# A fused attention, mixture-of-experts and GLU kernel: where the row list of the first expert is made

## The chip, the cores and the metric

The kernel runs on one core of one Trainium2 chip. The metric is the device time of one execution in microseconds (us). A core has a matrix engine (PE in the profile, with its weight loads as PEld), a vector engine (DVE), a scalar engine (ACT), GpSimd (POOL) and SyncE (SP), each with an instruction stream of its own. DMAs can be issued from the queues of SP, ACT and POOL.

## The reference

Inputs are q, k, v of 4 x 8 heads x 576 x 64, so 2304 tokens with 512 features. Everything is float32.

```python
kv  = einsum('bhsd,bhse->bhde', k, v)
x   = rmsnorm(einsum('bhsd,bhde->bhse', q, kv)) * g_norm   # 2304 x 512
noisy = x @ w_gate + log1p(exp(x @ w_noise)) * noise       # 8 experts
top2, weights = the two largest, softmax over these two
out[token] += weight * (relu(x @ w1[e]) @ w2[e])           # w1 512x1024, w2 1024x512
y = (sigmoid(out @ m2_gate) * (out @ m2_val)) @ m2_out     # width 1536
```

## The kernel before

The 2304 tokens are 18 tiles of 128. The attention stage makes one tile after the other; its raw rows go to a DRAM buffer `xbuf`. Routing is done for groups of tiles, `GROUPS = [(0, 5), (5, 8), (8, 13), (13, 18)]`: group 0 and 1 are "first", group 2 is `third` in the code, group 3 is `last`.

**The list.** Each token goes to two experts and has in each a slot number: a block `sb` (a column of 40, 5 blocks x 8 experts) and a place `rm` of 128 in the block. To gather the rows of a block, the kernel needs the list "which token stands at which place". It makes it by matmuls: for each tile i and choice j a one-hot `ohs[:, i, j]` (128 tokens x 128 places, by `rm`; this is the wide one) is multiplied with a one-hot `ovs[:, i, j]` (128 tokens x 40 columns, by `sb`) that has been multiplied with the token's number. The sum over all tiles in PSUM (`plist`) is the list; with a constant added it becomes `lsb`, whose columns are the row numbers of the indirect DMAs (`gather`). Both one-hots lie in one float16 tile, called `ohv` in the trace. A first, small list (`pfirst`, `lsa`) of groups 0 and 1 alone serves the first two blocks (`AB = 2`) of expert 0, so that expert 0 can begin while groups 2 and 3 are still routed. A third form, `lsq`, has four row numbers for each place (rows as quarters); it is made from the whole list by a copy (`lsf`), four small matmuls (`psq`) and one addition, and is what the gathers for expert 1 from its third block on and for all later experts read.

**Routing as a generator.** `route(g)` is cut by `yield` into 19 steps, for group 3: 1 is `rms_a`; 2 is ACT's Ln and Exp; 3 to 5 finish the norm `rms_y`, copy it beside the rows (POOL for group 3) and store rows; 6 and 7 are the logits (`Lr`, `lg`); 8 is ACT's Exp and Ln (`sp`); 9 to 11 find the two largest (`mk`); 12 and 13 rank them (`prk` on PE); 14 gives `sb` and `rm`; 15 to 17 make the one-hots; 18 and 19 the token's weights. `step(g, n)` runs n steps of group g at that place of the program, `advance(n)` n steps of all groups in work.

**Weight splits.** Weights are split in a high part (ACT) and a low part (DVE, which subtracts ACT's result). `work()` does the next split and loads the next raw weights: for expert 0, four pieces of w1 (`w_0h`, `w_0l` to `w_3h`, `w_3l`), then four of w2 of the same names. Each w1 piece is used by one call `h_first(p, 0)`, which multiplies the first two blocks (256 rows) with 256 columns of w1 in 24 matmuls (`ph`) and leaves the relu in high and low parts (`ha`; ACT, then DVE). Then two calls of `y_step` (24 matmuls each, `py`) multiply with w2, then the three blocks 2 to 4 come in: gather, scaling (`xs`, DVE), four transposes each (`pxT`), high part `xh` (ACT) and low part `xl` (DVE), and the second half of the first layer (`ph` with 368 columns).

**Order.** SP and POOL keep program order everywhere, ACT does up to the end of this part; PE and DVE are ordered by a scheduler from the program's priorities, except inside the `with in_order("PE DVE")` block, whose PE and DVE instructions keep their order among themselves. Steps of groups 1 and 3 have a higher priority (`URGENT`).

Before the block, PE does four idle products (`warm`, eight instructions) while the first gathers land. `free` holds tiles for split weights.

## Time and profile before

| | before |
|---|---|
| median of 3 runs | 944.24 us (944.13 to 947.38) |
| the profiled execution | 937.66 us |
| span of its instructions | 935.9 us |
| mean granted clock of PE | 0.996 |
| PE busy | 909.1 us (97%) |
| DVE busy | 682.3 us (73%) |
| ACT busy | 439.6 us (47%) |
| POOL busy | 383.6 us (41%) |

A row of the timeline gives start, duration, engine, line of the kernel, operation, what it writes and reads, and in brackets how long the engine had been idle before it and what ended that. Durations of neighbours on one engine overlap a little, so the cost of one among many is the distance of starts.

### The profile page before, as it was taken

The numbers are of one execution on the slowest core, as the hardware profiler recorded it, in microseconds if no ns is written. First come the engines' busy times: TensorE is split into PE (matmuls) and PEld (weight loads), VectorE is DVE, ScalarE is ACT, GpSimd is POOL, SyncE is SP. The second block draws the span as 40 slices with busy tenths as digits, with TensorE's granted clock in tenths as the row PEclk, the third lists the DMA queues.
The fourth block names the chain that finished last, engine by engine and source line by source line (L and its number), as shares of the span: only waits on it lengthen the run. The fifth ranks groups of instructions, "written<-read, shape, count | busy, mean of one in ns | idle before, by whom it ended". The sixth has DMA issues, their size and how long they took to land.

```text
span 935.9 us, 14318 instructions
## 1 busy us (share of the span) xinstructions
PE 909.1 (97%) x5157; PEld 788.7 (84%) x5157; DVE 682.3 (73%) x1025; ACT 439.6 (47%) x659; POOL 383.6 (41%) x378
## 2 busy tenths in 40 slices
PE   7888889999999999999999999999999999999998
PEld 4877779989798998989899898888888888888886
DVE  2489597877788687787967468987977767866463
ACT  1675254353434343424333687554654555544441
POOL 2142664737366383844600383333453636300000
PEclk9999999999999999999999999999999999999999
DMA  9986678777857566666744476696477777986784
GB/s 263 290 257 216 188 216 279 259 257 274 262 188 234 185 221 194 207 206 216 225 155 141 140 251 215 217 333 222 171 266 263 244 253 252 350 269 201 217 249 98
DMA packets 134379, 213.92 MB, mean 229 GB/s; under 512 B 20384, under 2 KB 65952, under 8 KB 134304
## 3 DMA queue, kind: packets, MB, share of 16 engines
q1 hardware_dynamic: 116496, 179.82, 59.7%
q0 software_dynamic: 7664, 20.26, 7.4%
q10 hardware_dynamic: 10144, 12.88, 4.1%
q8 instruction: 41, 0.67, 0.3%
q14 instruction: 34, 0.28, 0.1%
HBM read 140.94 MB, written 71.97 MB: 228 GB/s over the span
## 4 chain that ended last, share of the span: by engine, by line
PE 58%; DVE 5%; DMA 4%; ACT 2%; issue 2%; SPq 1%; POOL 0%; DVEq 0%; ACTq 0%
PE py L817 15%; PE ph L774 14%; PE pga L1174 8%; PE poa L1353 7%; PE pgc L1174 4%; PE poc L1353 3%; PE pgb L1174 2%; PE pout L1323 2%; PE pob L1353 2%; DMA xturn<-yg 1%; DMA yg<-ybuf,slot 1%; DVE wt L994 1%; DMA lw<-wbuf 1%; DMA yg<-xturn 1%; DVE xf L1072 1%
## 5 line engine op out<-in xcount | busy, mean ns | idle before, releaser
L714 POOL DMA_INDIRECT xg<-xbuf,lsq x132 | 152.8, 1158 | 51.2 <-issue 30.9
L994 DVE TENSOR_TENSOR wt<-lw,wt 128x512 fp32r<-128x512 f32 x84 | 69.9, 837 | 35.7 <-ACT wt L993 33.6
L778 ACT ACTIVATE hh<-ph 128x624 fp32r<-128x624 f32 (+1 forms) x60 | 41.4, 694 | 95.7 <-PE ph L774 93.9
L779 DVE SCALAR_TENSOR_TENSOR hl<-ph,hh 128x624 fp32r<-128x624 f32 (+1 forms) x60 | 48.7, 811 | 48.2 <-ACT hh L778 47.0
L714 POOL DMA_INDIRECT yg<-ybuf,slot x36 | 39.0, 1084 | 77.6 <-issue 57.7
L733 POOL TENSOR_TENSOR xg<-xg 128x512 f32<-128x512 f32 x33 | 36.5, 1107 | 40.3 <-DMA xg<-xbuf,lsq 35.2
L763 ACT ACTIVATE xh<-xT 128x512 fp32r<-128x512 f32 (+3 forms) x40 | 21.1, 543 | 66.6 <-DVE xT L760 65.4
L993 ACT ACTIVATE wt<-lw 128x512 fp32r<-128x512 f32 x84 | 49.9, 621 | 0.0
L1211 POOL TENSOR_TENSOR qt<-qv 128x512 f32<-128x512 f32 x12 | 19.7, 1642 | 68.9 <-DVE qv L1198 37.2
L1188 ACT ACTIVATE q<-pga 128x1024 f32<-128x1024 f32 x24 | 24.6, 1027 | 44.8 <-PE pga L1174 43.5
L764 DVE TENSOR_TENSOR xl<-xT,xh 128x512 fp32r<-128x512 f32 (+3 forms) x40 | 24.9, 634 | 27.0 <-ACT xh L763 27.0
L695 POOL COPY seen<-hh 128x1 f32<-128x1 f32 x42 | 16.8, 401 | 65.7 <-ACT hh L778 65.5
L774 PE MATMUL ph<-xh,w_3h 128*128 128x312 f32 (+2 forms) x128 | 39.3, 307 | 1.6 <-DVE hl L779 0.9
L774 PE MATMUL ph<-xh,w_3l 128*128 128x312 f32 (+2 forms) x128 | 39.3, 307 | 1.5 <-DVE w_3l L645 1.5
L774 PE MATMUL ph<-xl,w_0h 128*128 128x312 f32 (+2 forms) x128 | 39.1, 313 | 1.3 <-DVE xl L764 1.3
L822 ACT ACTIVATE yo<-py 128x512 f32<-128x512 f32 (+1 forms) x40 | 23.5, 588 | 35.6 <-PE py L817 32.7
L774 PE MATMUL ph<-xh,w_1l 128*128 128x312 f32 (+2 forms) x128 | 39.2, 307 | 0.7 <-DVE w_1l L645 0.7
L774 PE MATMUL ph<-xh,w_0l 128*128 128x312 f32 (+2 forms) x128 | 39.6, 312 | 0.3 <-PEq L852 0.3
L774 PE MATMUL ph<-xh,w_0h 128*128 128x312 f32 (+2 forms) x128 | 39.6, 312 | 0.0
L774 PE MATMUL ph<-xh,w_1h 128*128 128x312 f32 (+2 forms) x128 | 39.2, 306 | 0.0
L774 PE MATMUL ph<-xl,w_2h 128*128 128x312 f32 (+2 forms) x128 | 39.1, 306 | 0.0
L774 PE MATMUL ph<-xh,w_2h 128*128 128x312 f32 (+2 forms) x128 | 39.1, 306 | 0.0
(562 smaller groups left out, 3118.5 us busy)
## 6 DMA issues: line engine op xcount, KB each, us to landing
raw<-in_moe_w_dram SPq DMA_DIRECT2D x60, 512.0 KB, 4.8
lw<-wbuf SPq DMA_DIRECT2D x84, 256.0 KB, 4.1
gr<-qbuf SPq DMA_DIRECT2D x42, 512.0 KB, 4.7
ybuf<-yo ACTq DMA_DIRECT2D x32, 256.0 KB, 3.2
ybuf<-zero SPq DMA_DIRECT2D x29, 256.0 KB, 6.3
raw<-in_moe_w_out_dram SPq DMA_DIRECT2D x12, 512.0 KB, 5.5
raw<-in_moe_w_gate_dram SPq DMA_DIRECT2D x12, 512.0 KB, 4.8
raw<-in_moe_w_val_dram SPq DMA_DIRECT2D x12, 512.0 KB, 4.4
```

Of the source, the lines that this page charges most:

```text
L714: nc.gpsimd.indirect_dma_start(out=x, out_offset=None, in_=src, in_offset=bass.IndirectOffsetOnAxis(ap=ix, axis=0))
L733: eng.tensor_mul(xv, xv, x[:, :, 128:, None].to_broadcast([128, 4, KD, 32]))
L764: nc.vector.tensor_sub(XL[e, s][:, :, a:z], pt[:, :, o:o + z - a], XA[e, s][:, :, a:z].bitcast(FT))
L774: nc.tensor.matmul(ph, w[:, c, j], x[e, s][:, c, :], start=(n == 0), stop=(n == 3 * KD - 1))
L778: nc.scalar.activation(hh, ph, AF.Relu)
L779: nc.vector.scalar_tensor_tensor(hl, ph, 0.0, hh.bitcast(FT), op0=OP.max, op1=OP.subtract)
L817: nc.tensor.matmul(py[0:m], x[:, f % 2, t], w[:, f % 2, :], start=(n == 0), stop=(n == 3 * FC - 1))
L993: nc.scalar.activation(hi, src, AF.Copy)
L994: nc.vector.tensor_sub(lo, src, hi.bitcast(FT))
L1174: nc.tensor.matmul(ps[:, j, 0:HT[c]], w[:, a, k, s], x[:, k, :], start=(first and i == 0), stop=(i == 5), skip_group_check=not first)
L1188: nc.scalar.activation(q[name], src, AF.Copy)
L1353: nc.tensor.matmul(ps[:, j, 0:HT[c]], w, g[x][1][:, f, :], start=(first and u + f + i == 0), stop=(u == FP3 - 1 and f + i == 3), skip_grou ...
```

## The change

Four edits. (1) The token's number is multiplied into the wide one-hot `ohs` as the second operation of the instruction that makes it; the multiplication of `ovs`, an instruction of its own, goes. (2) The last group's wide one-hots are all made on DVE; before, three of the ten were POOL's. (3) In the program's order, the split of w1's second piece moves ahead of `step(third)` and the first steps of the last group inside the block, and the split of its fourth piece moves from behind `h_first(1, 0)` and steps 8 to 11 of the last group to ahead of them. In the same place step 8 of the last group moves behind `h_first(1, 0)`. (4) `lsf`, `psq` and `lsq` are made together with `lsb`, at its priority, before the rows of blocks 2 to 4 are scaled and brought in; before, they stood behind that.

```diff
@@ route
-                eng = nc.gpsimd if j and (g != len(groups) - 1 or i < 3) or not g else nc.vector
-                eng.tensor_scalar(ohs[:, i, j], i128[:, 0:128], rm[:, i, j:j + 1], None, op0=OP.is_equal)
+                eng = nc.gpsimd if j and g != len(groups) - 1 or not g else nc.vector
+                eng.tensor_scalar(ohs[:, i, j], i128[:, 0:128], rm[:, i, j:j + 1], tokid[:, t0 + i:t0 + i + 1],
+                                  op0=OP.is_equal, op1=OP.mult)
             if i == 1:
                 nc.vector.tensor_tensor(ovs[:, :n], i128[:, None, None, 0:NB * E].to_broadcast(shp),
                                         sb[:, :, :, None].to_broadcast(shp), op=OP.is_equal)
-                nc.vector.tensor_mul(ovs[:, :n], ovs[:, :n], tokid[:, t0:t1, None, None].to_broadcast(shp))
@@ main program
         nc.tensor.matmul(pw, qT[NT - 1][:, 0], qT[NT - 1].rearrange("p h d -> p (h d)"), start=True, stop=True)
+        work()
         step(third)
-        step(last, 2)
-        work()
-        step(last)
+        step(last, 3)
         h_first(0, 0)
     work()
     step(third)
     step(last, 4)
     step(third, 2)
-    step(last)
+    work()
     h_first(1, 0)
-    step(last, 3)
+    step(last, 4)
     step(third)
-    work()
     h_first(2, 0)
@@
         for blk in range(AB, NB):
             gather(0, blk)
+        lsf = sml.tile([128, NB * E], HF, name="lsf")
+        nc.vector.tensor_copy(lsf, pl)
+        psq = pa([128, 4, NB * E], "psq")
+        for b in range(4):
+            nc.tensor.matmul(psq[:, b], sel[:, b], lsf, start=True, stop=True)
+        nc.vector.tensor_scalar(lsq, psq, quarter, 4.0 * TOK, op0=OP.add, op1=OP.add)
     for blk in range(AB, NB):
         scale(0, blk, nc.vector)
@@
-    lsf = sml.tile([128, NB * E], HF, name="lsf")
-    nc.vector.tensor_copy(lsf, pl)
-    psq = pa([128, 4, NB * E], "psq")
-    for b in range(4):
-        nc.tensor.matmul(psq[:, b], sel[:, b], lsf, start=True, stop=True)
-    nc.vector.tensor_scalar(lsq, psq, quarter, 4.0 * TOK, op0=OP.add, op1=OP.add)
```

## Rows read from the trace of the kernel before

**Rows 1.** Busy time by stretch: us, then PE, PEld, DVE, ACT, POOL, PEclk, DMA, GB/s.
```profile
70.00:91.00 21.00, 17.88 (x128) 14.58 (x127) 19.00 (x69) 9.97 (x18) 6.29 (x10) 1.00 0.75 238
...
300.00:500.00 200.00, 200.00 (x1151) 181.82 (x1150) 153.69 (x217) 77.15 (x114) 96.32 (x98) 1.00 0.62 200
```
**Rows 2.** Timeline of PE, 74 to 112 us: the matmuls that began after a wait.
```profile
79.66 0.39 PE L774 MATMUL ph<-xh,w_1l 128*128 128x256 f32 x1 [0.72 <-DVE w_1l L645]
...
86.07 0.36 PE L774 MATMUL ph<-xh,w_3h 128*128 128x256 f32 x1 [0.63 <-DVE dn L550]
...
88.03 0.38 PE L774 MATMUL ph<-xh,w_3l 128*128 128x256 f32 x1 [1.49 <-DVE w_3l L645]
...
96.92 0.29 PE L1432 MATMUL plist<-ohv 128*128 128x40 f16 x5 [1.32 <-POOL ohv L539]
...
106.55 0.63 PE L756 MATMUL pxT<-ident,xs 128*128 128x128 f32 x4 [0.58 <-DVE xs L720]
...
109.47 0.43 PE L774 MATMUL ph<-xl,w_0h 128*128 128x368 f32 x1 [1.06 <-DVE xl L764]
```
**Rows 3.** Timeline of ACT, 74 to 108 us: the splits and what stands ahead of them.
```profile
76.73 0.24 ACT L446 ACTIVATE rms_y<-rms_a 128x40 f32<-128x40 f32 x1 [2.02 <-DVE rms_a L443]
...
84.63 1.14 ACT L644 ACTIVATE w_3h<-raw,gcol 128x1024 fp32r<-128x1024 f32 x1
...
106.17 1.59 ACT L763 ACTIVATE xh<-pxT 128x512 fp32r<-128x512 f32 x3 [0.44 <-PE pxT L756]
```
**Rows 4.** Timeline of DVE, 74 to 110 us.
```profile
78.31 1.28 DVE L645 SCALAR_TENSOR_TENSOR w_1l<-raw,gcol,w_1h 128x1024 fp32r<-128x1024 f32 x1 [1.25 <-ACT w_1h L644]
...
94.54 0.27 DVE L539 TENSOR_SCALAR ohv<-i,rm 128x128 f16<-128x128 f16 x1
94.71 0.56 DVE L543 TENSOR_TENSOR ohv<-ohv,tokid 128x400 f16<-128x400 f16 x1
95.19 0.16 DVE L554 TENSOR_SCALAR dn<-dn 128x5 f32<-128x5 f32 x1
...
97.25 0.20 DVE L1520 TENSOR_SCALAR lsb<-plist 128x40 int32<-128x40 f32 x1 [0.77 <-PE plist L1432]
...
105.71 0.69 DVE L720 TENSOR_TENSOR xs<-xg 128x512 f32<-128x512 f32 x1 [1.63 <-DMA xg<-xbuf,lsb]
107.31 0.38 DVE L1540 TENSOR_SCALAR lsq<-psq,quarter 128x160 int32<-128x160 f32 x1 [0.91 <-PE psq L1539]
107.61 1.81 DVE L764 TENSOR_TENSOR xl<-pxT,xh 128x512 fp32r<-128x512 f32 x3
```
**Rows 5.** Tile ohv: POOL's instructions, ns min/median/max, first and last start.
```profile
L539 POOL TENSOR_SCALAR ohv<-i,rm x21: 590/612/2310, 56.5 to 94.7; 128x128 f16<-128x128 f16 x21
```
**Rows 6.** Timeline of POOL: the one-hots.
```profile
56.52 9.05 POOL L539 TENSOR_SCALAR ohv<-i,rm 128x128 f16<-128x128 f16 x13 [13.76 <-DVE rm L530]
...
93.35 3.52 POOL L539 TENSOR_SCALAR ohv<-i,rm 128x128 f16<-128x128 f16 x3 [4.39 <-DVE ohv L541]
```
**Rows 7.** Groups by line and shape, POOL and DVE: near kin of the two-operation form.
```profile
L695 POOL COPY seen<-q 128x1 f32<-128x1 f32 x5 | 1.6, 310 | 0.0
...
L288 DVE TENSOR_SCALAR sel<-sel 128x512 f16<-128x512 f16 x1 | 0.3, 285 | 0.0
```
**Rows 8.** Timeline, 69 to 74 us: the first two blocks come in.
```profile
71.66 0.69 DVE L720 TENSOR_TENSOR xs<-xg 128x512 f32<-128x512 f32 x1 [0.58 <-DMA xg<-xbuf,lsa]
...
73.00 1.04 PE L756 MATMUL pxT<-ident,xs 128*128 128x128 f32 x8
```
**Rows 9.** PE behind the join: one stretch (columns as above), then matmuls of two paces.
```profile
110.00:115.00 5.00, 5.00 (x23) 5.00 (x22) 1.60 (x10) 0.00 (x0) 3.78 (x5) 0.66 1.06 345
...
110.08 0.51 PE L774 MATMUL ph<-xl,w_0h 128*128 128x368 f32 x1
...
113.46 0.34 PE L774 MATMUL ph<-xh,w_0h 128*128 128x368 f32 x1
...
113.80 0.33 PE L774 MATMUL ph<-xh,w_0l 128*128 128x368 f32 x1
```

## The prediction

> **What bounds the kernel now.** I read the busy times by stretch first. From 300 to 500 us PE is busy for 200.00 of 200.00 us, while between 70 and 91 us it is busy for 17.88 of 21 [rows 1]. So PE is the clock of the program, and time is to be had where PE waits; a microsecond won ahead of such a full stretch is carried to the end. The second view is the timeline of PE over the place of the change, read for waits [rows 2]. Six waits stand there: 0.72 us for the low part of w1's second piece, 0.63 and 1.49 for the fourth piece, 1.32 for one-hots of POOL in the middle of the whole list, 0.58 for rows of the last block, 1.06 for low parts `xl`. The reader should see that they fall in two families: late weight splits, and late list (the last two hang on it).
>
> Third, ACT and DVE. ACT took up the second piece only after `rms_a` came from DVE (2.02 us idle), and the fourth piece's high part at 84.63 [rows 3]; DVE idled 1.25 us for the former [rows 4]. Apart from that DVE is busy for 19.00 of the 21 us [rows 1]: it is nearly full, and what comes later on its list can only be earlier if something is taken from it. POOL's last three one-hots began at 93.35 and took 3.52 us [rows 6]; DVE was through its own with the instruction at 94.54 [rows 4]. `lsb` followed at 97.25, the last `xs` at 105.71, `xl` began at 107.61 [rows 4], PE went on at 109.47 [rows 2]. This last chain is what I think sets the join with expert 0's second half.
>
> **The sum, part by part.** It is made against the profiled execution, 937.66 us, whose span is 935.9. The runs' median, 944.24, lies 6.6 above it; I carry the difference over unchanged.
>
> *Token number in the wide one-hot.* On DVE a one-hot costs 0.17 us (start at 94.54, next instruction at 94.71) and the multiplication that goes 0.48 (94.71 to 95.19) [rows 4]; there are four of these, two after 74 us, so 0.96 goes. The two-operation form on DVE isn't in the trace at this shape. From below it costs nothing more, from above the 0.17 again; the nearest row, `sel` with two operations on four times the elements, took 285 ns [rows 7], so I take nothing.
>
> On POOL the form isn't there either. One operation took 590 ns undisturbed [rows 5]. Bounds for the second: 0, and 590 again. A copy of a single element took 310 [rows 7], so at most 280 is the work on elements and scalar; I take a third of that, 0.1. Thirteen instructions lie in a row ahead of the first list (56.52 to 65.57) [rows 6], so 1.3 us. From it I take some 0.3, an estimate from these 13, which took 9.05 against 13 x 0.59 = 7.7: part of the 1.4 of disturbance lay beside the multiplications that go. So the first rows come 1.0 us later. What hides it: PE's idle products end at 73.00, when the second block's scaling (71.66 plus 0.69) is 0.65 old, and that block's transposes come half of 1.04 behind the first block's [rows 8]: 1.17 us of cover. Cost 0 at my value; each further 0.1 us of the price costs 1.3.
>
> The Trainium skill, in the GPSIMD Engine Reference (Performance versus the Vector engine, Elementwise), says that a loop with up to two operations per element is bound by the port, so that the second would be free. By that the first rows would come 0.3 earlier and nothing of my sum would change, since the idle products hide either; no row here shows a second operation on POOL.
>
> *Last group's one-hots on DVE.* Adds 3 x 0.17 = 0.51 to DVE, takes away 3.52 of POOL and the 1.32 of PE's wait.
>
> *Splits moved.* The second piece's high part now follows `xh` on ACT without waiting for `rms_a`: PE's 0.72 and DVE's 1.25 idle go. It is ahead of the last group's Ln and Exp, which wait for it by 1.1 to 1.2 on DVE too (the block keeps order), but then find the 1.28 of that split [rows 4] already behind them, so the group loses nothing. The fourth piece can follow the third on ACT, near 80 us, instead of 84.63 [rows 3]: 0.63 and 1.49 go. Its load of the next raw weights still stands behind the same row stores on SP, some us earlier.
>
> *Now the list.* DVE's end of the last one-hot was 94.71. Less 1.25 idle, less the third group's 0.48, plus 0.51: 93.5. The ten list products, 0.3, and a semaphore: `lsb` near 94.0 instead of 97.25, 3.2 us earlier. Against that, a split of w2 (its high part on ACT is earlier too) can now slip in front of the one-hots on DVE at some 1.2. I take 3.0 earlier, between 2.0 and 3.5. The gathers, scaling and transposes follow at their old distances.
>
> *Quarter list.* DVE sat 0.91 idle for `psq` and spent 0.30 on `lsq` while the first `xh` were ready; the last `xh` was through at 107.76 (106.17 plus 1.59) [rows 3], so its `xl` could have ended at 107.8 plus 0.65, 108.45, and not at 109.42 (107.61 plus 1.81) [rows 4]. That is 1.0 more. The new place costs DVE the same 0.5 at a time when w2's splits wait for it; PE covers that, see below. It also lets POOL go on with the gathers for expert 1 without waiting for `lsq` (107.31 plus 0.38), as fast as their buffers come free: some us more lead than PE has gained, so POOL's scaling of these rows meets other splits on DVE than before. I book neither gain nor loss for that; a price for it can't be read from this trace, and the range takes it in.
>
> Together 3.0 + 1.0 = 4.0 us at PE's 109.47. Is PE there in time? Without 0.72, 0.63, 1.49 and 1.32 of waiting it ends `y_step` 4.2 us earlier, before the rows are ready; so the list sets the join, and PE keeps some 2 us of idle time there. 937.66 - 4.0 = 933.7 for a profile like this, **940.2** for the median.
>
> **The rivals.**
>
> *The clock comes back too.* Behind the join PE's granted clock falls to 0.66 from 110 to 115 us, so the lower level of 1.2 GHz for part of it: eleven matmuls from 110.08 to 113.46 are 0.307 us apart, later ones 0.17 [rows 9], 1.5 us lost. Ahead of it PE had idled for over 2 us in pieces [rows 2]. If less idling keeps the clock up, the gain is 4.0 + 1.5 = 5.5, or more where DVE's later splits also fall clear of POOL: 938.5. Against: by my sum PE idles as long as before.
>
> *DVE takes it back.* The w2 splits, high parts ready earlier, push into every gap of the last group's chain on DVE: two of them ahead of the one-hots, 2.4 us, and PE waits for their remaining fellows as well. Then the list gains 1, the quarter list 1: 942.2. For it: DVE is the fullest engine here. Against: the last group's steps have the higher priority.
>
> *POOL's second operation is dear.* At 0.2 to 0.4 us the first rows come 2.3 to 4.9 late, 1.1 to 3.7 above the cover: 941.4 to 944.
>
> *Slower: it costs another whole instruction.* At 0.59 the 13 one-hots are 7.7 late, 7.4 net, 6.2 behind cover; the 4.0 stay: 946.4. It decides from (4.0 + 1.17 + 0.3) / 13 = 0.42 us on. Against it stands the 310 ns copy, which says that half of the instruction is fixed.
>
> **How the numbers follow.** Forecast 0.38 (3.0 to 5.0 gained), clock 0.27, DVE 0.20, dear POOL 0.10, slower 0.05. What can be told from no change is 0.5%, 4.7 us, beside runs that spread over 0.34%. Over 4.7 gained: all but little of the clock's 0.27 and a third of the forecast's 0.38, so 0.39. Slower by over 4.7 needs more than 0.9 us for POOL's second operation, or a new stall of that size: 0.04. The rest, 0.57, is within. For the range, the low end lets the clock's case win all of PE's six waits, 5.8, and 1.5, with a little for DVE's later collisions: 936.0. The high end leaves out the upper half of dear POOL and the slower case: 944.0.
>
> **What would show it.** Right: `w_1l` before 77.5 us and no wait of PE for `w_1l` or `w_3l`; all ten last one-hots on DVE, `lsb` between 93.5 and 95.5; `lsq` before the first `xs`; `xl` without `lsq` in front, PE on `xl` products near 105.5; POOL's one-hots 0.6 to 0.7. Wrong: POOL's one-hots at 0.8 or more with `pxT` beginning after 73; w2 splits between the last group's `rm` and its one-hots; a later stretch that gives the 4 us back, seen as new waits of PE between 110 and 160 us.

## The result and the profile after

| | before | after |
|---|---|---|
| median of 18 runs each | 944.99 us (939.59 to 953.41) | 950.19 us (947.69 to 957.11) |
| ratio | | 1.0055, interval 1.0038 to 1.0073 |
| the profiled execution, its span | 937.66, 935.9 us | 952.17, 950.4 us |
| mean granted clock of PE | 0.996 | 0.985 |

The change makes the kernel 5.2 us slower; 4.0 us faster had been forecast. Run again on two occasions, on a chip each, it gave 1.0041 (1.0014 to 1.0068) and 1.0015 (0.9994 to 1.0037), so by the ratios it is slower by 5.2, 3.9 and 1.4 us, and the last time not clearly slower at all. (The kernel before has medians from 938 to 946 us on the five chips used below, each of them used on one occasion. Every ratio is against runs of the kernel before on the same chip.)

First the one-hots (DVE's six in a row in the kernel before, for comparison, stand below): the tile `ohv` in the kernel after (ns min/median/max, first and last start), then the row of POOL's timeline with the 13 ahead of the first list.

```profile
L539 POOL TENSOR_SCALAR ohv<-i,rm,tokid x18: 784/790/1799, 56.9 to 90.1; 128x128 f16<-128x128 f16 x18
L539 DVE TENSOR_SCALAR ohv<-i,rm,tokid x18: 299/320/323, 63.9 to 98.2; 128x128 f16<-128x128 f16 x18
```
```profile
56.88 11.05 POOL L539 TENSOR_SCALAR ohv<-i,rm,tokid 128x128 f16<-128x128 f16 x13 [13.87 <-DVE rm L530]
```

POOL's second operation costs 0.19 us (least values 784 and 590 [rows 5]; medians 0.18), and the 13 take 2.00 us longer [rows 6]. On DVE the last group's six in a row take 1.43 us where six took 1.10 before: 0.05 each.

What these 2 us do on PE, first in the kernel before, then in the kernel after (the last product of the first list, the idle products, the first transposes; the last row is DVE's scaling of the second block):

```profile
65.62 0.18 PE L1432 MATMUL pfirst<-ohv 128*128 128x2 f16 x1 [0.37 <-POOL ohv L539]
69.56 3.60 PE L1482 MATMUL warm<-qT 128*128 128x512 f32 x8
```
```profile
67.99 0.18 PE L1432 MATMUL pfirst<-ohv 128*128 128x2 f16 x1 [0.57 <-POOL ohv L539]
72.67 3.60 PE L1482 MATMUL warm<-qT 128*128 128x512 f32 x8
76.10 1.04 PE L756 MATMUL pxT<-ident,xs 128*128 128x128 f32 x8
```
```profile
74.22 0.69 DVE L720 TENSOR_TENSOR xs<-xg 128x512 f32<-128x512 f32 x1
```

The products of the first list stand in PE's order ahead of attention's last products (`po`) and wait for POOL's one-hots: four waits of 2.15 us in all, where there were two of 0.64. So the idle products themselves begin later, and the transposes right behind them. The rows are not what PE waits for: they are scaled at 74.91, 1.2 us before the transposes begin.

The timeline of DVE in the kernel after, where the whole list is made:

```profile
92.01 1.22 DVE L648 TENSOR_TENSOR w_0l<-raw,w_0h 128x1024 fp32r<-128x1024 f32 x1
...
94.09 0.17 DVE L526 TENSOR_SCALAR qi<-ri 128x10 int32<-128x10 int32 x1
...
94.24 1.23 DVE L648 TENSOR_TENSOR w_1l<-raw,w_1h 128x1024 fp32r<-128x1024 f32 x1
95.37 0.17 DVE L528 SCALAR_TENSOR_TENSOR sb<-qi,ee 128x10 f32<-128x10 int32 x1
95.45 0.17 DVE L530 SCALAR_TENSOR_TENSOR rm<-qi,ri 128x10 f32<-128x10 int32 x1
...
96.08 1.43 DVE L539 TENSOR_SCALAR ohv<-i,rm,tokid 128x128 f16<-128x128 f16 x6
...
97.49 0.99 DVE L539 TENSOR_SCALAR ohv<-i,rm,tokid 128x128 f16<-128x128 f16 x4
...
98.46 1.23 DVE L648 TENSOR_TENSOR w_2l<-raw,w_2h 128x1024 fp32r<-128x1024 f32 x1
99.59 0.20 DVE L1518 TENSOR_SCALAR lsb<-plist 128x40 int32<-128x40 f32 x1
...
100.94 0.39 DVE L1526 TENSOR_SCALAR lsq<-psq,quarter 128x160 int32<-128x160 f32 x1
```

The same place in the kernel before:

```profile
90.19 1.22 DVE L648 TENSOR_TENSOR w_0l<-raw,w_0h 128x1024 fp32r<-128x1024 f32 x1
...
92.62 0.16 DVE L530 SCALAR_TENSOR_TENSOR rm<-qi,ri 128x10 f32<-128x10 int32 x1
...
93.25 1.10 DVE L539 TENSOR_SCALAR ohv<-i,rm 128x128 f16<-128x128 f16 x6
...
95.26 1.21 DVE L648 TENSOR_TENSOR w_1l<-raw,w_1h 128x1024 fp32r<-128x1024 f32 x1
```

The reader should see how many splits of w2 stand ahead of `rm`: before it was `w_0l` alone, now it is `w_0l` and `w_1l`. Before, `w_1l` stood behind all one-hots, in time for which DVE had to wait for POOL's anyway [rows 6]; now it stands between `qi` and `rm`, at 1.1 us. (`w_2l`, behind the one-hots, costs nothing: PE's last list product ends at 99.52.) `lsb` comes at 99.59 instead of 97.25 [rows 4].

PE at the join, from its timeline in the kernel after: what began after a wait, then the products behind it.

```profile
107.05 0.63 PE L756 MATMUL pxT<-ident,xs 128*128 128x128 f32 x4 [1.32 <-DVE xs L720]
109.99 1.09 PE L756 MATMUL pxT<-ident,xs 128*128 128x128 f32 x4 [2.31 <-issue]
...
111.71 0.67 PE L774 MATMUL ph<-xh,w_0h 128*128 128x368 f32 x1 [0.60 <-issue]
...
113.50 0.68 PE L774 MATMUL ph<-xl,w_0h 128*128 128x368 f32 x1 [0.82 <-DVE xl L764]
113.98 0.51 PE L774 MATMUL ph<-xh,w_0l 128*128 128x368 f32 x1
...
119.50 0.34 PE L774 MATMUL ph<-xh,w_0l 128*128 128x368 f32 x1
119.67 0.33 PE L774 MATMUL ph<-xh,w_0h 128*128 128x368 f32 x1
```

The same place by stretch (columns as in rows 1), kernel after:

```profile
105.00:110.00 5.00, 1.37 (x11) 0.88 (x9) 1.41 (x3) 1.79 (x3) 3.78 (x5) 0.93 0.92 281
110.00:115.00 5.00, 3.58 (x13) 2.95 (x14) 3.54 (x17) 0.54 (x1) 3.78 (x5) 0.50 0.69 224
115.00:120.00 5.00, 5.00 (x19) 5.00 (x18) 0.27 (x2) 0.00 (x0) 4.51 (x5) 0.55 1.00 315
```

PE waits at four places and is idle for 5.05 of the 10 us from 105 on; in the kernel before it was 2.11 (busy 2.89 and 5.00). The granted clock is 0.50 from 110 to 115, the lower level of 1.2 GHz throughout, and mostly so to 120. So 18 steps of 0.307 us follow `xl` (113.98 to 119.50) where there had been 11 [rows 9]: 7 x 0.14 = 1.0 us more.

Since single executions differ by some us ahead of the change, I compare stages by their distance from one event, the first rank product of group 0 (`prk<-mk,tri` on PE, near 54 us). Each number is a start read from a timeline, less that event; `py` is the first product with w2, `xs` the end of the last scaling, `xl` the first product with `xl`, `hh` the high part of a hidden layer (the first, 9th, 25th and 57th on ACT, of 60 of all experts), `end` the last instruction.

```
kernel                    py     rm    lsb     xs     xl    hh 1   hh 9  hh 25  hh 57    end
before                  37.12  38.71  43.34  52.49  55.56  61.3  110.5  222.6  441.7  882.0
before, again (r5)      39.85  41.43  46.07  55.54  58.62  64.3  113.5  227.8  448.8  891.6
after                   37.32  41.18  45.32  55.57  59.23  67.3  116.2  227.9  446.9  896.1
after, third time (r17) 38.39  42.26  46.41  56.82  60.43  66.1  113.2  224.8  443.8  885.6
second operation (e1)   40.34  42.43  47.08  56.03  59.11  66.1  114.8  227.3  446.3  892.1
splits (e2)             34.66  38.55  43.12  53.13  56.20  62.9  110.6  222.3  441.3  889.5
quarter list (e3)       37.53  39.12  43.75  52.61  57.50  66.7  116.6  227.7  446.7  892.8
quarter list (r15)      38.46  40.05  44.68  54.23  57.48  61.6  109.4  221.3  441.1  883.1
list first (r8)         34.53  37.13  40.94  49.11  56.78  62.5  110.9  222.4  441.4  882.2
no quarter list (r13)   37.29  41.15  45.30  56.15  59.72  66.3  114.6  226.0  444.9  886.3
after + idle (r18)      37.31  41.17  45.32  55.74  58.04  62.2  108.8  222.5  441.5  883.8
splits + idle (r16)     34.90  38.79  42.82  53.17  55.46  59.5  106.4  220.9  440.0  883.2
```

By this table the kernel after has lost 2.0 us at `lsb`, 3.1 at `xs`, 3.7 at `xl`, 6.0 at the first `hh`, 5.7 at the 9th, and 5.2 still at the 57th. That this equals the loss of the medians is partly luck. Each row is one execution, and the first profile of before is 7 us under its own median and among the earliest of its kind: r5, the same kernel, is 7.1 later at the 57th and 2.7 at `lsb`. Firmer is the comparison of groups. Seven profiles with the old order of splits and one operation (before, r5, r7, e3, r12, r14, r15) have `lsb` at 43.3 to 46.1, on average 44.6, and `xs` at 54.0 on average; seven with moved splits and the second operation (after, r6, r9, r10, r13, r17, r18) have `lsb` at 44.7 to 46.4, on average 45.3, and `xs` at 55.7. So the list is in none of them 3 us earlier; it is later by about 0.8, and the last rows by 1.7. (These are different chips; the groups were put together after the fact.)

The first of these profiles and the kernel after differ by more at their ends: the two spans differ by 14.5; the other 9 arise behind the 57th `hh`. They are not the change's: splits alone (e2), level with before in its median, take 448.2 us from there to the end, the changed kernel on another chip (r17) 441.8, and before 440.3.

A second measure uses all runs: span x (1 - mean granted clock) is the part of a span that the lower clock took away. It is an upper bound of what it cost, as it counts idle time too. The rest is span x granted clock. Means in us, with those of before on the same chip in brackets (for the first comparison these are not on record; the kernel after has 12.0 and 936.9 there):

```
kernel                             ratio (95%)                lower clock     rest
after, again (r9)                  1.0041 (1.0014 to 1.0068)  10.9 (6.9)   937.0 (937.4)
after, third time (r17)            1.0015 (0.9994 to 1.0037)   7.9 (5.0)   931.2 (932.4)
after + idle, chip of r17 (r18)    1.0020 (0.9997 to 1.0042)   5.1 (5.0)   934.2 (932.4)
after + idle (r6)                  1.0003 (0.9982 to 1.0024)   4.5 (4.0)   932.7 (933.0)
after + idle, chip of r9 (r10)     1.0085 (1.0053 to 1.0118)  10.2 (6.9)   942.2 (937.4)
without the quarter list (r13)     1.0041 (1.0017 to 1.0065)   8.0 (4.3)   932.3 (932.2)
without the second operation (e4)  1.0028 (1.0007 to 1.0049)  10.3 (7.1)   936.7 (937.5)
second operation alone (e1)        1.0017 (0.9995 to 1.0038)   8.2 (7.1)   938.0 (937.5)
splits alone (e2)                  1.0002 (0.9976 to 1.0028)   7.6 (7.1)   937.2 (937.5)
quarter list alone (e3)            1.0032 (1.0010 to 1.0054)   8.2 (7.1)   939.5 (937.5)
quarter list alone (r15)           1.0000 (0.9977 to 1.0022)   4.5 (4.3)   932.1 (932.2)
quarter list, lsq late (r14)       0.9987 (0.9968 to 1.0007)   4.5 (4.3)   931.8 (932.2)
quarter list + counts (r12)        1.0028 (1.0005 to 1.0051)   7.0 (6.9)   940.3 (937.4)
before + idle (r7)                 0.9999 (0.9978 to 1.0021)   3.5 (4.0)   932.9 (933.0)
list first (r8)                    0.9998 (0.9978 to 1.0018)   6.1 (4.0)   930.9 (933.0)
several (r11)                      1.0001 (0.9974 to 1.0028)   5.1 (6.9)   940.1 (937.4)
splits + idle (r16)                1.0034 (1.0013 to 1.0055)   5.6 (4.3)   934.3 (932.2)
```

### The profile page after: what moved, and what is told of

Its sections match the earlier page's. It is cut to its first block, busy times and chain, and to the rows that moved or that the text cites. A ratio compares the mean times of both kernels' runs of the same rounds, so it can differ in the third digit from the quotient of the medians.

```text
span 950.4 us, 14310 instructions
## 1 busy us (share of the span) xinstructions
PE 918.7 (97%) x5155; PEld 796.4 (84%) x5157; DVE 678.8 (71%) x1024; ACT 441.0 (46%) x659; POOL 387.6 (41%) x375
## 4 chain that ended last, share of the span: by engine, by line
PE 66%; DVE 2%; issue 2%; DMA 1%; ACT 0%; POOL 0%; ACTq 0%; DVEq 0%; POOLq 0%
PE py L817 14%; PE ph L774 14%; PE pga L1174 13%; PE poa L1353 7%; PE pgc L1174 6%; PE poc L1353 3%; PE pgb L1174 3%; PE pgv L1142 2%; PE pob L1353 2%; PE pout L1323 1%; DMA out_dram<-o 1%; DMA yg<-ybuf,slot 0%; DVE wt L994 0%; DMA lw<-wbuf 0%; DVE xf L1072 0%
## 5 line engine op out<-in xcount | busy, mean ns | idle before, releaser
L733 POOL TENSOR_TENSOR xg<-xg 128x512 f32<-128x512 f32 x33 | 38.7, 1175 | 36.6 <-DMA xg<-xbuf,lsq 30.0
L774 PE MATMUL ph<-xl,w_3h 128*128 128x312 f32 (+2 forms) x128 | 39.8, 311 | 0.0
L774 PE MATMUL ph<-xh,w_2l 128*128 128x312 f32 (+2 forms) x128 | 39.2, 306 | 0.4 <-DVE w_2l L645 0.4
L774 PE MATMUL ph<-xl,w_1h 128*128 128x312 f32 (+2 forms) x128 | 39.2, 306 | 0.0
```

The costliest lines, as they stand in the source:

```text
L733: eng.tensor_mul(xv, xv, x[:, :, 128:, None].to_broadcast([128, 4, KD, 32]))
L774: nc.tensor.matmul(ph, w[:, c, j], x[e, s][:, c, :], start=(n == 0), stop=(n == 3 * KD - 1))
```

## The experiments

**The parts alone (e1 to e4, one chip).** e1 is before with the token number moved into the one-hots:

```diff
-                eng.tensor_scalar(ohs[:, i, j], i128[:, 0:128], rm[:, i, j:j + 1], None, op0=OP.is_equal)
+                eng.tensor_scalar(ohs[:, i, j], i128[:, 0:128], rm[:, i, j:j + 1], tokid[:, t0 + i:t0 + i + 1], op0=OP.is_equal, op1=OP.mult)
-                nc.vector.tensor_mul(ovs[:, :n], ovs[:, :n], tokid[:, t0:t1, None, None].to_broadcast(shp))
```

> Only the token number moves into the wide one-hots; the last group's split over DVE and POOL, the splits' order and the quarter list stay as before. Theory A (POOL's second operation is the loss: 0.2 us more on each of 13 one-hots ahead of the first list, PE's products of that list stand in its queue ahead of attention's last tiles, so expert 0 starts some 3 us later, and the clock takes more behind the join): 3 to 6 us slower than before, transposes of the first two blocks begin near 76 us instead of 73.0. Rival B (the early quarter list is the loss, by expert 1's gathers that run beside the last gather of expert 0): within 1.5 us of before. Rival C (the moved splits are the loss): within 1.5 us of before.

e2 is before with the two splits moved as in the change:

```diff
+        work()
         step(third)
-        step(last, 2)
-        work()
-        step(last)
+        step(last, 3)
...
-    step(last)
+    work()
     h_first(1, 0)
-    step(last, 3)
+    step(last, 4)
     step(third)
-    work()
```

> Only the two splits (and step 8 of the last group) move. Theory A: PE's waits for w_1l and w_3l go (0.72, 0.63, 1.49 us), the list doesn't come earlier by as much, 0 to 3 us faster than before. Rival B: the same, 0 to 3 faster. Rival C: 2 to 5 us slower, with the last group's rm on DVE later than 92.8 us.

e3 is before with only `lsf`, `psq` and `lsq` made with the whole list, e4 the whole change without the second operation:

```diff
             gather(0, blk)
+        lsf = sml.tile([128, NB * E], HF, name="lsf")
...
+        nc.vector.tensor_scalar(lsq, psq, quarter, 4.0 * TOK, op0=OP.add, op1=OP.add)
     for blk in range(AB, NB):
         scale(0, blk, nc.vector)
```

> Only the quarter list is made with the whole list. Theory A: 0 to 2 us faster, since xl no longer waits behind lsq (PE goes on at 108.5 instead of 109.5 us). Rival B: 2 to 5 us slower; the last block's rows land 1 us or more later than 3.6 us after their gather's end, and the matmuls behind the join run at half pace for longer. Rival C: within 1 us of before.

> The whole change without the move of the token number: ovs is multiplied as before, one operation per wide one-hot, the last group's ten on DVE, splits and quarter list as in the change. Theory A: expert 0 starts at the old time (transposes at 73.0), and the sum of the prediction holds without its POOL term: 2 to 5 us faster than before. Rival B: 1 to 4 us slower than before. Rival C: 0 to 4 us slower than before.

Measured 1.0017, 1.0002, 1.0032 and 1.0028. In e1 the first transposes come 2.2 us later by the event (21.27 against 19.08) and the list 3.7 (`rm` 42.43 against 38.71, `lsb` 47.08 against 43.34): POOL makes all 21 of its one-hots at 0.79 us, and PE still waits 1.36 us for the last. That cost far less than the 3 to 6 us expected. In e2 PE is 2.5 us earlier at the first product with w2 (34.66 against 37.12), but `rm` only 0.16 and `lsb` 0.22. The timeline of DVE in e2 shows the order of the kernel after:

```profile
93.22 0.17 DVE L526 TENSOR_SCALAR qi<-ri 128x10 int32<-128x10 int32 x1
...
93.37 1.22 DVE L648 TENSOR_TENSOR w_1l<-raw,w_1h 128x1024 fp32r<-128x1024 f32 x1
94.50 0.17 DVE L528 SCALAR_TENSOR_TENSOR sb<-qi,ee 128x10 f32<-128x10 int32 x1
94.58 0.17 DVE L530 SCALAR_TENSOR_TENSOR rm<-qi,ri 128x10 f32<-128x10 int32 x1
```

So beside the first profile of before the splits buy PE 2.5 us and the list next to nothing (beside the average of the seven, 44.6, the list is 1.5 earlier, half of what was forecast). PE is at the join earlier and waits there longer, busy for 1.72 of the five us from 105:

```profile
105.00:110.00 5.00, 1.72 (x16) 1.21 (x15) 1.38 (x2) 1.79 (x4) 1.67 (x2) 1.00 0.79 243
110.00:115.00 5.00, 3.46 (x14) 3.13 (x13) 4.27 (x19) 0.51 (x1) 3.37 (x4) 0.61 0.79 245
115.00:120.00 5.00, 5.00 (x24) 5.00 (x23) 0.23 (x1) 1.04 (x2) 3.78 (x5) 0.71 0.80 261
```

Behind it 17 steps are at half pace, nearly as in the kernel after, and yet e2 is level with before, so these steps are not enough for the loss.

e4 contradicts the forecast most directly. Without the second operation expert 0 starts at the old time (transposes at 19.11 by the event) and the list is early (`lsb` 42.58), as its theory A asked, but the last `xs` is at 52.79, `xl` at 56.45, and the kernel is 0.28% slower and not 2 to 5 us faster. So the second operation is not the whole loss. The last group's one-hots on DVE (the second edit) have no run of their own; they are in e4, r13 and r16, which are slower, and in r8 and r11, which are level.

**Level of the profile (r5), idle products (r6, r7), list first (r8), one chip.** r5 is the kernel before once more. r6 is the kernel after with idle products of PE in front of the transposes of the three gathered blocks (6, 6, 3) and of the `xl` products (4); r7 the same in before (0, 0, 2 and 5). They write to tiles that are overwritten behind them.

```diff
             pt = pa([128, KD, 128], "pxT")
+            if e == 0 and blk >= AB:
+                for _ in range((6, 6, 3)[blk - AB]):
+                    nc.tensor.matmul(pt, sel[:, 0], sel, start=True, stop=True)
```

r8 has the splits moved, the last group's one-hots on DVE and the quarter list early, without the second operation; DVE keeps to an order in which the list goes ahead of the splits of w2, and the counts stand right behind it:

```diff
-    advance(4)
-    for blk in range(AB):
-        y_step(0, blk, lambda f: advance(1))
+    with in_order("DVE"):
+        advance(4)
+        while routes:
+            advance(1)
+        for blk in range(AB):
+            y_step(0, blk)
```

> The kernel before, unchanged, for a second profile of it. The first profile, 937.66 us, lies under all 35 later runs of the same kernel (941.92 to 951.33), and it has no stall of PE between 500 and 600 us, where every other profile of this case has 3 to 6 us. Theory A (that stall and the lower clock there come and go with the run, whatever the kernel): a profile at 944 to 948 us, PE short of 100 us by 3 to 5 between 500 and 600 us, and after the join the same stages as in the first profile within 0.5 us, with the half clock from about 110 to 113.5 us. Theory B (the stall belongs to the changed kernels): again 937 to 940 us and PE at 99.9 of 100 us there.

> The changed kernel with idle products on PE at the join, whose results are overwritten: 6, 6 and 3 of 512 columns ahead of the transposes of blocks 2, 3 and 4 and 4 ahead of the first product of the second half; they take about 4.2 us of the 5.1 that PE waits there and hold up nothing that is not waiting for rows. In the runs so far the share of the span that the lower clock took is 12.0 us for the changed kernel (mean over 18 runs of span times one minus granted clock) and 7.1 for the one before, while the rest of the span is 936.9 against 937.5. Theory A (the loss of 5.2 us is the clock that falls because PE idles longer at the join): the half clock behind the join goes, 20 products at 0.307 us become products at 0.167, and the time falls by 3 to 5 us to 945 to 947. Theory B (the loss is lateness of the list itself and the collisions of later splits with GpSimd): the time stays at 949 to 951 although the clock is up.

> The kernel before with idle products at the join: 2 of 512 columns ahead of the transposes of block 4, where PE waited 0.58 us, and 5 of 368 columns ahead of the first product of the second half, in the 1.06 us in which PE waited for low parts. Theory A (idling at the join sets the clock behind it, and 1.6 us of idling is already enough to lose it): the half clock from 110 to 113.5 us goes and 1.5 us come back, 0.2% faster than before. Theory B (the clock there does not hang on these gaps): no change, between 0.1% faster and 0.1% slower.

> The kernel before with the parts of the change that touch neither GpSimd's one-hots nor their second operation (two splits moved forward, last group's ten one-hots on VectorE, quarter list with the whole list), and two more: VectorE keeps the written order from the last group's rank on, so that the splits of the second, third and fourth piece of w2 stand behind the one-hots and not in front, and the counts per expert (pcnt) are taken with the list, so that they no longer stand in front of the low parts xl. Theory A (the forecast's 3 us were lost because splits of w2 slipped in front of the last group's one-hots): the rows rm come 37.0 to 37.5 us after the first rank product (38.55 with the splits moved alone), lsb at 40 to 41 (before 43.34, with the change 45.32), last xs at 49 to 50.5 (before 52.49). PE then waits 4 to 5 us for the second piece of w2 in the middle of the y products, so the join itself comes at 53.5 to 55 (before 55.56), and the time is 0 to 2 us under before if the clock holds through that wait, 0 to 2 above if it falls. Theory B (something else holds the list, such as the rank product or ACT): lsb not under 42.5.

r5's single run, 947.71 us, is some 3 us behind the first profile of the same kernel from `py` to the 9th `hh`, and more later: that is the scatter of one execution, and differences of 3 us between two rows of the stage table don't bear a verdict by themselves. r6 is level with before (1.0003; the kernel after was not run on this chip), r7 too (0.9999), though the eleven products at half pace behind the join are gone in r7. r8 shows what had been forecast for the list: `lsb` 2.4 us earlier than before, `xs` 3.4. But now PE's work with w2 is short of weights. From the timelines of ACT, then of PE, in r8:

```profile
95.00 0.21 ACT L552 ACTIVATE dn<-dn 128x5 f32<-128x5 f32 x1 [6.34 <-DVE dn L550]
95.11 1.04 ACT L647 ACTIVATE w_1h<-raw 128x1024 fp32r<-128x1024 f32 x1
```
```profile
96.20 0.73 PE L817 MATMUL py<-w_1h,ha 128*128 128x512 f32 x2 [0.42 <-ACT w_1h L647]
...
97.72 0.50 PE L817 MATMUL py<-w_1l,ha 128*128 128x512 f32 x1 [0.78 <-DVE w_1l L648]
```

ACT keeps program order, and its Exp for the last group waits 6.34 us for DVE, with the high part of w2's second piece behind it. `xl` is at 56.78, no earlier than before, and the time is the same. In this order the list is early and the weights are late. That both can't be had isn't shown: what ACT waits for is one small instruction (`dn`), which this order puts behind the one-hots (94.80 on DVE, 85.84 in before).

**The change again with and without idle products, and two mixtures (r9 to r12, another chip).** r9 is the kernel after, r10 the kernel of r6. r11 is r8 without the fixed order, with 0, 4, 3 and 4 idle products and with the stores of the first two y blocks issued behind the raw loads. r12 is e3 with the counts right behind the list, ahead of the `xs`.

```diff
+    with tc.high_priority():
+        pc = pa([128, E], "pcnt")
+        ...
+        nc.vector.tensor_copy(cnt[:, E:2 * E], base)
     for blk in range(AB, NB):
         scale(0, blk, nc.vector)
```

> The changed kernel, unchanged, beside the same with idle products (the run below) on one chip, since the kernel before has had medians of 945 and 946 us on two occasions and 938.6 on a third. Theory A (the loss is the clock behind the join): 0.4 to 0.7% slower than before here too, the half clock for 6 us or more behind the join, and some 4 to 5 us more of it in the whole span than the kernel before (mean of span times one minus granted clock). Theory B (the loss belongs to the occasion of the first comparison): within 0.2% of before.

> The changed kernel with the idle products at the join once more, now beside the changed kernel itself. Theory A: 3 to 5 us under the changed kernel, so within 0.2% of before, with no half clock between 105 and 125 us; the first product of low parts at 57 us after the first rank product (59.2 without idle products), hh of the second half at 61 (67.3). Theory B: no difference from the changed kernel beyond 1 us.

> What the runs so far favour, put together: two splits moved forward, last group's ten one-hots on VectorE with one operation each (the multiplication of the narrow ones stays), quarter list and counts with the whole list, the y rows of blocks 0 and 1 stored behind the second half's xh on ACT's queue (so that they do not land among the gathers), and idle products on PE (0, 4, 3 ahead of the transposes of blocks 2, 3, 4, and 4 ahead of the first product). Theory A (list, then clock): lsb at 42.6 us after the first rank product as with the one-operation runs, last xs at 51 (before 52.5), low parts' first product at 53.5 to 54.5 (before 55.6 to 58.6), no half clock behind it, and 2 to 4 us under before. Theory B (what the list wins is given back by later splits that meet GpSimd's scaling): the join is as early, but expert 1 starts (first hh of 624 columns) no earlier than 95 us, and the time stays within 1 us of before.

> The quarter list made with the whole list, as in the run of that part alone, and the counts per expert taken there too, so that they no longer stand in front of the low parts xl on VectorE. Alone, the early quarter list lost 0.32% (0.10 to 0.54), with the low parts' first product 4.9 us behind the last xs (before 3.07). Theory A (the counts, which took the quarter list's place in front of xl, cost it): xl right behind the xh, the first product of low parts 2.5 us or less behind the last xs, and 0.0 to 0.2% faster than before. Theory B (GpSimd's earlier gathers and scaling for expert 1 cost it): still 0.2 to 0.4% slower, with a split of expert 1 stretched to over 3 us beside GpSimd's scaling.

The change loses again (1.0041). The idle products, level on the chip before, are worse here (1.0085, six runs). One place where the lead at the join goes stands in the timelines of ACT and PE in r10:

```profile
123.29 0.78 ACT L781 ACTIVATE hh<-ph 128x736 fp32r<-128x736 f32 x1 [12.43 <-PE ph L777]
```
```profile
125.08 0.44 PE L777 MATMUL ph<-xh,w_2h 128*128 128x368 f32 x1 [3.16 <-DVE hl L782]
```

PE's last product for this `hh` had ended at 115.87; ACT took it up 7.4 us later, and PE then waited 3.16 us for `hl`. The same is seen, at 1.2 to 5.6 us, in after, r9, e1, e3, e4, r11 and r12, so in three of the six comparisons; in the others, and in e2, `hh` follows its product within 0.04 us. The three are those in which before has a median of 945 to 946 us; in the others it has 938 to 940. This doesn't account for all of r10's loss: at the 9th `hh` its profile is level with that of r9 again (116.0 and 116.7). r12 puts the counts out of the way (`xs` to `xl` 2.83 us, where e3 has 4.89) and is no better (1.0028, on another chip than e3), so the counts weren't what e3 lost by. r11, the mixture, is level (1.0001): its list comes at 44.49, not at the 42.6 expected, and its `hh` is late.

**Taking the quarter list out, or only its gathers (r13 to r16, another chip).** r13 is the kernel after with the quarter list at its old place; r14 is before with `lsf` and `psq` made early and `lsq` written late, r15 repeats e3; r16 is r13 without the second operation, with 0, 4, 3 and 4 idle products. The diff is r14's.

```diff
             gather(0, blk)
+        lsf = sml.tile([128, NB * E], HF, name="lsf")
...
+            nc.tensor.matmul(psq[:, b], sel[:, b], lsf, start=True, stop=True)
...
+    nc.vector.tensor_scalar(lsq, psq, quarter, 4.0 * TOK, op0=OP.add, op1=OP.add)
     pc = pa([128, E], "pcnt")
```

> The whole change, but with the quarter list at its old place. Theory A (each part has its own price, and the early quarter list carries some 3 us of the loss, as quarter-only's ratio of 1.0032 says): 1.0015 to 1.0025, about 1.5 to 2.4 us slower than before, no late hh0 (from the end of phxl to hh0 under 7.2 us), the rest is POOL's second operation. Theory B (the loss is the longer idling of PE ahead of the join, whatever the quarter list does): 1.004 to 1.0055, as the whole change.

> Before, with lsf and the four products for the quarter list made with the whole list, but with lsq written by DVE at the old place, so that the gathers for expert 1 can't start early. Theory A (what the early quarter list costs comes from expert 1's gathers, which then run beside the loads on ACT's queue and hold hh0 back): 0.9985 to 1.0005, hh0 at once behind its product. Theory B (it comes from DVE's and PE's work at the new place and from the counts that go ahead of xl): 1.002 to 1.0035.

> The quarter list alone, again, as the measure for the two kernels above on this chip. If the loss is the kernel's: 1.002 to 1.0045 with hh0 2 us or more behind its product. If it depends on the chip: 0.999 to 1.001, with hh0 at once behind its product, and then the other ratios of this call are to be read beside that.

> Splits moved and the last group's one-hots on DVE, without the second operation and with the quarter list at its old place; besides, PE does idle products ahead of the transposes of the second and third gathered block and ahead of the xl products (4, 3 and 4). Theory A (the splits do win PE's waits, and the lower clock behind the join took them back): 0.997 to 0.9985, no stretch at 1.2 GHz between 105 and 125 us, from pxT to the first w2 output 2 us less than in before. Theory B (the list sets the join, so the splits win nothing even at the full clock but the 1.5 us that the idle products give): 0.9985 to 1.0005.

On this chip the quarter list costs nothing (r15 1.0000, `hh` 0.04 us behind its product), so r14 can't say which half of it cost 0.3% elsewhere. From ACT's timeline, e3 and then r15, the same program:

```profile
120.72 0.78 ACT L778 ACTIVATE hh<-ph 128x736 fp32r<-128x736 f32 x1 [12.33 <-remote]
```
```profile
115.72 0.79 ACT L778 ACTIVATE hh<-ph 128x736 fp32r<-128x736 f32 x1 [6.04 <-DMA raw<-in_moe_w_dram]
```

r13 loses 4 us (1.0041) with no late `hh` and no early gathers, so second operation, moved splits and the last group's one-hots on DVE are enough for it. By the parts' own prices it should have been 1.0015 to 1.0025. By stretch, r13:

```profile
105.00:110.00 5.00, 1.97 (x12) 1.08 (x10) 1.23 (x2) 1.79 (x3) 2.00 (x3) 0.99 0.89 253
110.00:115.00 5.00, 2.55 (x13) 1.94 (x14) 3.14 (x10) 0.54 (x1) 1.52 (x2) 0.50 0.39 131
115.00:120.00 5.00, 5.00 (x17) 5.00 (x17) 1.82 (x12) 0.00 (x0) 3.78 (x5) 0.50 1.08 359
```

Beside the first profile of before the list is 2.0 us later and PE's first product with w2 level (`py` 37.29 and 37.12); beside r14 on the same chip the list is 0.6 later and PE 1.2 earlier. PE idles for 5.48 of the 10 us from 105, and the clock is 0.50 from 110 to 120. The lower clock's part of the span is 3.7 us above that of before, and the mean span 3.9.

r16 looks best at the join (`xl` 55.46, 9th `hh` 106.4) and is slower (1.0034). Its lead over r14 melts from 3.0 us at the 9th `hh` (109.4 there) to 0.4 at the 25th. One place of it, PE's timeline in r16:

```profile
237.22 0.39 PE L823 MATMUL py<-w_3h,hl 128*128 128x512 f32 x1
239.42 0.50 PE L823 MATMUL py<-w_0h,hh 128*128 128x512 f32 x1 [1.81 <-ACT yo L828]
...
240.30 0.63 PE L823 MATMUL py<-w_0h,hh 128*128 128x512 f32 x1
240.73 0.63 PE L823 MATMUL py<-w_0l,hh 128*128 128x512 f32 x1
```

PE waits 1.81 us for ACT's copy `yo` of an earlier block, and falls to the lower clock right behind (products 0.43 us apart, 0.23 ahead of it). The kernel before has a wait for `yo` too, 1.77 us at 253.00, without the fall. Kernels that come later mostly wait less there (between 200 and 300 us r14 1.3, r13 1.0, after 1.4 in all). What is won at the join is partly waited off here: r16 waits 0.5 us more than r14 and has seven products behind it at 0.43 us for 0.23, 1.4 us more.

**The pair on one chip (r17, r18).** The kernel after, and the kernel of r6.

> The changed kernel, once more, as the measure for the kernel below on the same chip. Both theories: 1.003 to 1.0055, three stretches at 1.2 GHz in the profile before 125 us or so, the one at the join some 10 us long; the share of the span that the lower clock takes is 3 to 5 us above that of before.

> The changed kernel with idle products in PE's gaps ahead of the join (6, 6, 3 ahead of the transposes of the three gathered blocks and 4 ahead of the xl products). They add no work to another engine. Theory A (the loss is the lower clock behind a join for which PE waits longer): 0.999 to 1.0015, 3 to 5 us less than the changed kernel beside it, no stretch at 1.2 GHz from 100 to 125 us. Theory B (the loss is something else that the lower clock goes with, as the late list and the early gathers): within 1.5 us of the changed kernel, or above it as in the first such pair (1.0085 beside 1.0041).

By stretch, r18, to be read beside the kernel after:

```profile
105.00:110.00 5.00, 5.00 (x26) 3.17 (x25) 1.42 (x2) 1.51 (x3) 3.78 (x5) 1.00 0.82 221
110.00:115.00 5.00, 3.68 (x24) 2.79 (x22) 3.56 (x14) 1.14 (x2) 3.78 (x5) 1.00 0.71 235
```

r17 came out better than both theories had it: 1.0015, with nine products at half pace behind the join. In r18 the clock stays at 1.00, `xl` to `hh` takes 4.1 us instead of 5.7, and the 9th `hh` is 4.4 us earlier than in r17. Of this 1.1 was there at `py`, ahead of the idle products (37.31 and 38.39), so 3.3 can be theirs. At the 25th 2.3 are left (PE's wait for `yo` between 200 and 300 us is 2.1 us in r18, 1.2 in r17), at the end 1.8, and the medians agree (941.22 and 940.82). The lower clock's part falls by 2.8 us as expected; the rest grows by 3.1. (The spans of the two profiles, 939.5 and 940.0, hide the 1.8: r18's reached the event 2.3 us later, 56.21 against 53.92, ahead of all that is changed.) So the theory that the lower clock is the loss, to be had back by keeping PE busy, fails on the time though each of its signs came.

## Why the prediction was wrong, point by point

**"I take 3.0 earlier, between 2.0 and 3.5" is the step that failed**, and with it "Cost 0 at my value" for the first list. Measured, no profile with the change has the list earlier than the average of the old order, and the kernel after has it 2.0 us later than the first profile of before. Four things make up the lateness at the join.

- *The cover for the first list did not exist.* The prediction took the end of PE's idle products, 73.00, as fixed, with 1.17 us of cover behind it. But those products stand behind the products of the first list in PE's order, and come later with them: 72.67 instead of 69.56, 2.7 later by the event, and `pxT` as much. The rows themselves were ready 1.2 us before it. This shows in every profile: the last product of the first list is 11.7 to 11.8 us behind the event in the twelve with one operation and 13.6 to 13.8 in the eight with two, and `pxT` 19.1 to 19.2 and 21.2 to 22.9.
- *The list wins less than forecast from the splits.* The sum subtracted DVE's idle time and the removed instructions from the old time of `lsb`, as if the rest of DVE's work kept its place. In the kernel after, the last group's `mk` is 1.7 us late, so 1.0 of the 2.7 has been won back; then one more split of w2 (`w_1l`, 1.1 us) stands ahead of `rm`, which is 2.5 late. From `rm` to `lsb` it needs 0.5 less. e2 shows the same order of splits without the late first list, and r8 that 2.4 to 3.4 us are there when the order is forced.
- *"The gathers, scaling and transposes follow at their old distances"* failed by 1 us: from `lsb` to the end of the last `xs` the kernel after takes 10.25 us, before 9.15. In the ten profiles in which the second store of `y` rows (`ybuf<-yo`, on ACT's queue) is issued 6.1 to 6.5 us behind `lsb`, the last scaling begins 9.3 to 10.2 behind it; in the ten in which that store is issued at 8.5 or later, 7.5 to 8.9. The gather of these rows is issued at the same distance in both (3.7 to 4.6). So the stores of `y`, which the moved splits bring forward, fit as the cause. r11, which has the moved splits but puts these stores off, has 8.0; it differs in more than that, so the cause is not isolated.
- *From `xs` to `xl`* it takes 3.66 us, before 3.07: the counts stand there where `lsq` stood, and the last four transposes take 1.09 us at the lower clock, before 0.63 [rows 2]. In r18, with the clock up, it is 2.30.

The rival "DVE takes it back" named the second of these. It took two further splits ahead of the one-hots and a gain of 1 us left over; it was one split, and no gain was left because of the first. The sign that the prediction gave for it, splits between `rm` and its one-hots, looked at the wrong place: they stand ahead of `rm`.

How these make 5.2, 3.9 and 1.4 us is not settled. r13 (without the quarter list) and e4 (without the second operation) are slower too, and the later join alone, 3.7 us beside the first profile, is no firmer than single executions are.

**"POOL's second operation at 0.1"** was 0.19, and 2.0 us for the 13. The bounds (0 and 0.59) held; a third of 280 ns was too low, and the rival "dear" began at what was measured. By the Trainium skill (GPSIMD Engine Reference, Performance versus the Vector engine, Elementwise) a loop of up to two operations per element is bound by the port. That the second would then be free did not come true: 590 ns with one operation and 784 with two, on the same 128 x 128 elements, and the measurement decides. Whether the 0.19 lies in the loop or in the fixed part of the instruction no run here tells, as there is only one size. e1 prices the whole at 1.0017, not clearly different from nothing.

**The second operation on DVE, taken as nothing,** was 0.05 us each, 0.5 for the last group's ten, which is the 0.48 of the multiplication that went.

**PE's waits of 0.72, 0.63 and 1.49 us were to go,** and went. None of them is in the trace after (waits of 0.38, 0.57 and 0.31 came up instead, for `w_2l`, `mk` and w2's `w_0l`), and e2 has PE 2.5 us earlier for it.

**"The list sets the join, and PE keeps some 2 us of idle time there"** was half right: the list does set it, and PE idled for 5.05 us from 105 to 115, since PE came no later (`py` 0.2) and the rows 3.1. So the rival "the clock comes back" turned into its opposite: 18 steps at half pace instead of 11, some 1.0 us, besides the lower clock earlier and later on.

**The quarter list, "1.0 more",** was wrong in its gain: the counts took `lsq`'s place in front of `xl` (`cf` at 111.15, `xl` at 111.64 in the kernel after), so nothing of the 1.0 came. That its gathers start earlier was foreseen and left without a price. On one chip e3 cost 3 us, with `hh` 3.5 us behind its product; on another the same program cost nothing (r15; the intervals of the two, 1.0010 to 1.0054 and 0.9977 to 1.0022, overlap).

**The slower rival** asked for 0.42 us at POOL's second operation. That price was never reached. It came slower although the second operation cost less than that, because the 4.0 us on the other side of the balance did not exist, nor the cover of 1.17.

**What stays open.** Why `hh` on ACT comes late on some chips: no transfer or instruction in these traces is seen to hold it, and e3 and r15 are the same program. But a transfer can't be ruled out: of the 16 parts of each of ACT's loads ahead of this `hh`, the traces in which it is late hold the landing of at most 7, where those of r13 to r17 hold all (e2 holds as few and has no late `hh`). Whether the chip is what differs, or the occasion, is open too, as each chip was used on one occasion. And why the kernels with idle products, ahead at the join and, in r16 and r18, with no half pace behind it, are not faster in the median: a wait and slow products that take back 1.9 us of the lead are shown in r16, a longer wait in r18, the rest isn't.

## What to carry to other kernels

On an engine that is 90% busy, work brought forward lands in front of something: before booking the gain, list what will stand ahead of the critical chain in the new order. When something is said to be hidden behind work that ends at a fixed time, ask what that work itself waits for. Two streams that meet at a join must gain together. Moving the earlier one forward alone buys idle time, and here idle time on PE was often, not always, followed by products at half pace; it can also bring that stream's stores forward among the other's loads. And a lead won in one stage may be waited off at the next shared buffer; look for the wait further on that grows with the lead.

## What the runs showed of the hardware

- A compare on POOL (128 x 128 float16) takes 590 ns at least, with a multiplication by a second per-partition scalar 784 (medians 612 and 790); on DVE the distance of starts goes from 0.17 to 0.22 us.
- Products of 368 columns follow each other at 0.167 us at the full clock and at 0.307 at the lower level. From 105 to 115 us, around the fall, PE idled for 5.05 in after and 5.48 in r13. The idle time alone doesn't tell: between its last product with w2 and the first with `xl` PE idled for 2.1 us in before, with eleven products at half pace behind, and for 2.6 in r14 and r15, with none.
- The same program against the same base came out differently on different chips: the whole change 1.0015 (0.9994 to 1.0037) to 1.0055 (1.0038 to 1.0073), the quarter list alone 1.0000 and 1.0032 with intervals that overlap.
